# PSUM tiles of a fused attention, gating and mixing kernel: two Vh tiles or two y transposes to one pair of banks, the short Vh tile in one bank, rank-32 additions ahead of the statistics

## The chip, the cores and the metric

The kernel runs on one core of one Trainium2 chip. The core has a matrix engine (TensorE, PE in the profile, with its weight loads as PEld), VectorE (DVE), ScalarE (ACT), GpSimd (POOL) and a queue that issues the DMAs (SyncE, SP). Each engine works through its own instructions in order and waits on semaphores for the others. The metric is device microseconds (us) of one execution. Before the change three executions gave 1314.13, 1310.84 and 1314.26 us, the median 1314.13 us.

## The reference

Eight batches of 576 rows and 512 columns go through three blocks, all in fp32:

- linear attention: `q_s` and `k_s` are softmaxes (of q along the head's 64 columns, of k along the 576 rows), `kv = k_s.T @ v` for each of 8 heads, `x = q_s @ kv`;
- a gated block: `h = gelu(x @ w_in)`, split into `u` and `v` of 512 columns each; `v` is normalised along its columns (mean and variance, then `g_ln`), mixed along the rows by `w_sg` with the bias `b_sg`, multiplied by `u`, sent through `w_out` and added to `x`; call the result `y`;
- a mixing block: `u2 = y + (y.T @ U @ V).T`, where U is 576 by 32 and V is 32 by 576 (the rank-32 addition), and `out = u2 + relu(u2 @ w_ch1) @ w_ch2`.

## The kernel before

fp32 products are made of three matmuls of reduced-precision operands (a high and a low part of each side). `prod` issues the three for both halves of 288 columns, `mm` is one matmul. Every operand therefore has a copy (high part, mostly ACT) and a subtraction (low part, DVE or POOL).

The first part loops over the batches b = 0 to 7. For each b the matrix engine does, in this order: the Vh tiles (`emit_Vh`, the second half of `x @ w_in`, five row tiles t = 0 to 4, the last with 64 rows), mixed with what is left of batch b-1: the transposes of its `y` (`emit_yT`, tile 2 after Vh 0, tiles 3 and 4 after Vh 1), its product with U (`emit_U`, after Vh 2) and the rank-32 addition (`emit_PV`, column blocks 0 and 1 after Vh 3, 2 and 3 after Vh 4); then the maximum over k for batch b+1 (`k_max`, transposes into `pm`), four blocks of `emit_Uh` with `k_spread` (two matmuls into `pb`) ahead of the third, four of `emit_S` (the mixing along the rows), `emit_kv` and `emit_qT` of batch b+1, four of `emit_y`, and `emit_xT` of batch b+1. The second part, from about 634 us on, is the big product with `w_ch1` and `w_ch2`, in a scheme with seven products in place of eight.

After Vh of a tile, ACT applies gelu (L616) into `ge`; `stats` (L622 to L630) takes mean and variance on DVE and the power -0.5 on POOL; `emit_ln` (L632 to L647) makes `sh` on DVE (L636), the normalised tile on ACT (L639), its high part `vh` on ACT and its low part `vl` on POOL. For the short tile a copy of 64 rows (L618) and a DVE addition come before gelu (L620). `emit_ln` of tile t-1 comes after `stats` of tile t. `k_max` makes `mx` from `pm` on DVE (L425), `mh` and `ml` from it, and two `diag` tiles on POOL (DVE for the first batches) which `k_spread` multiplies.

PSUM has eight banks of 2 KB a partition. The pool `ps2` holds three tiles of two banks (tag "big"), `ps1` two tiles of one bank. A new tile takes the place of the one three (or two) allocations before it, and its first matmul waits until all readers of that one are done. Before the change every Vh tile and the y transposes of tiles 2 and 3 take one whole "big" place each, though they fill one of its banks. The order in ps2 for b > 0 is: Vh 0, yT 2, Vh 1, yT 3, Vh 2, Vh 3, addition 0, addition 1, Vh 4, addition 2, addition 3, Uh 0.

The orders of PE (whole kernel) and of DVE (inside the loop) are as written in the program. The orders of ACT, POOL and SP inside the loop are chosen by a planner that simulates the program when it is built; it may put a later instruction of the program ahead of an earlier one that isn't ready. `behind(dve)` only places the k and q maxima behind an earlier DVE instruction.

Of the kernel before, what the change touches and what calls it, by code (L numbers as in the profile page):

```python
# [8 lines left out]
F32 = mybir.dt.float32  # L9
# [13 lines left out]
def fused_kernel(tc, q, k, v, w_in, g_ln, w_sgT, b_sg, w_out, U, V, w_ch1, w_ch2, outT):  # L23
    nc = tc.nc
    B, S, C = q.shape
    P = 128
    H, D = 8, 64
    NT = S // P
    R = S - NT * P
    NC = C // P  # L30
    F = w_out.shape[0]
# [19 lines left out]
    def mm(out, lhsT, rhs, first, last, onto=False):  # L51
        pe.matmul(out, lhsT, rhs, start=first, stop=last, skip_group_check=onto)  # L52

    def tt(eng, out, a, b, op):
        return eng.tensor_tensor(out=out, in0=a, in1=b, op=op)  # L55
# [4 lines left out]
    def copy(out, src):  # L60
        return act.activation(out, src, AF.Copy)  # L61

    def low(eng, out, src, hi):
        return tt(eng, out, src, as_f32(hi), ALU.subtract)

    def opened(name, bufs=1, **kw):
        cm = tc.tile_pool(name=name, bufs=bufs, reuse_waits="tile", **kw)
        return cm.__enter__(), lambda: cm.__exit__(None, None, None)
# [8 lines left out]
    ps2, close_ps2 = opened("ps2", 3, space=PSUM)  # L77
    ps1, close_ps1 = opened("ps1", 2, space=PSUM)
# [22 lines left out]
    half = cst.tile([P, 1], F32, name="half")  # L101
# [360 lines left out]
    def q_max(b, t):  # L462
        if t == 0:
            q_s[b] = tmpp.tile([P, NT + 1, H], F32, tag="qm", name="qm")
        dve.tensor_reduce(
            out=q_s[b][0 : TR[t], t], in_=q3(t), op=ALU.max, axis=mybir.AxisListType.X
        )
# [79 lines left out]
    def halves(t):  # L547
        return t[:, :, 0:HS]

    def two(ap):  # L550
        return ap.rearrange("p (j n) -> p j n", n=HS)
# [10 lines left out]
    def behind(eng):  # L562
        return tc.issue_after(last[eng].ins)
# [31 lines left out]

    vh = {}
    ln = {}

    def emit_Vh(b, t):
        xh, xl, xr, _ = x_t[b]  # L600
        pv = ps2.tile([P, 1024], F32, tag="big", name="pv")[:, 0:F]
        wv_h, wv_l = wi[1]
        for kc in range(NC):
            if t < NT:
                a, l = xh[:, kc, t * P : (t + 1) * P], xl[:, kc, t * P : (t + 1) * P]
                mm(pv, a, wv_h[:, kc], kc == 0, False)
                mm(pv, a, wv_l[:, kc], False, False)
                mm(pv, l, wv_h[:, kc], False, kc == NC - 1)
            else:
                a = xr[:, kc].rearrange("p j r -> p (j r)")  # L610
                mm(pv, a, wv_h[:, kc], kc == 0, False)
                mm(pv, a, wv_l[:, kc], False, kc == NC - 1)
        ge = tmpp.tile([P, F], F32, tag="ge", name="ge", bufs=3)
        ln[b, t] = ge
        if t < NT:
            act.activation(ge, pv, AF.Gelu_apprx_tanh)  # L616
        else:
            copy(ge[0:R], pv[64 : 64 + R])  # L618
            tt(dve, ge[0:R], pv[0:R], ge[0:R], ALU.add)
            act.activation(ge[0:R], ge[0:R], AF.Gelu_apprx_tanh)  # L620

    def stats(b, t):  # L622
        ge, n = ln[b, t], TR[t]
        bst = tmpp.tile([P, 6], F32, tag="bst", name="bst", bufs=3)
        mv = tmpp.tile([P, 2], F32, tag="mv", name="mv", bufs=3)
        dve.bn_stats(out=bst[0:n], in_=ge[0:n])  # L626
        dve.bn_aggr(out=mv[0:n], in_=bst[0:n])
        dve.tensor_scalar(out=mv[0:n, 1:2], in0=mv[0:n, 1:2], scalar1=1e-6, scalar2=None, op0=ALU.add)
        tt(pool, mv[0:n, 1:2], mv[0:n, 1:2], half[0:n], ALU.pow)
        ln[b, t] = (ge, mv)  # L630

    def emit_ln(b, t):  # L632
        ge, mv = ln.pop((b, t))
        n = TR[t]
        shift = tmpp.tile([P, 1], F32, tag="sh", name="sh", bufs=4)
        dve.scalar_tensor_tensor(  # L636
            out=shift[0:n], in0=mv[0:n, 0:1], scalar=-1.0, in1=mv[0:n, 1:2], op0=ALU.mult, op1=ALU.mult
        )
        act.activation(ge[0:n], ge[0:n], AF.Identity, bias=shift[0:n], scale=mv[0:n, 1:2])  # L639
        h = wrk.tile([P, F], F32R, tag=f"vh{t}", name=f"vh{t}")  # L640
        if t < NT:
            l = wrk.tile([P, F], F32R, tag=f"vl{t}", name=f"vl{t}")
            copy(h, ge)
            low(pool, l, ge, h)
            vh[b, t] = (h, l)
        else:
            copy(h[0:R], ge[0:R])  # L647
            low(dve, h[64 : 64 + R], ge[0:R], h[0:R])
            vh[b, t] = h
# [57 lines left out]
    def emit_yT(b, t):  # L707
        n = TR[t]
        if t not in (2, 3) or b == B - 1:
            pt = ps1.tile([P, C], F32, tag="ps1", name="pt1")  # L710
        else:
            pt = ps2.tile([P, 1024], F32, tag="big", name="pt1")[:, 0:C]
        for c in range(NC):
            pe.transpose(pt[0:n, c * P : (c + 1) * P], y_t[b][:, c, t * P : t * P + n], ident)  # L714
        h = wrk.tile([P, C], F32R, tag=f"vh{t}", name=f"yh{t}")
        if t < NT:
            l = wrk.tile([P, C], F32R, tag=f"vl{t}", name=f"yl{t}")
            copy(h, pt)
            low(dve, l, pt, h)
            yn[b, t] = (h, l)  # L720
        else:
            copy(h[0:R], pt[0:R])
            low(dve, h[64 : 64 + R], pt[0:R], h[0:R])
            yn[b, t] = (h,)
# [5 lines left out]
    def emit_U(b, t):  # L730
        if t == 0:
            pu_t[b] = ps1.tile([P, C], F32, tag="ps1", name="pp")
        parts = yn.pop((b, t))
        w = u_w[:, t].rearrange("p a r -> p (a r)")
        for i, y in enumerate(parts):
            mm(pu_t[b], w, y, t == 0 and i == 0, t == NT and i == len(parts) - 1)
        if t == NT:
            pp = pu_t.pop(b)
            if b < B - 1:
                s = tmpp.tile([P, S], F32R, tag="gt", name="pst")[:, 0:C]  # L740
            else:
                s = wrk.tile([P, C], F32R, tag="xr", name="pst")
            copy(s, pp)
            low(dve, s[3 * RK : P], pp[3 * RK : P], s[3 * RK : P])
            pu_t[b] = s
# [10 lines left out]
    def emit_PV(b, c):  # L756
        s = pu_t[b][:, c * P : (c + 1) * P]
        pw = ps2.tile([P, 2, 512], F32, tag="big", name="pw")
        for j in range(2):
            mm(pw[:, j, 0:HS], s, v_w[:, j * HS : (j + 1) * HS], True, True)  # L760
        y = y_t[b][:, c]
        tt(dve, two(y), halves(pw), two(y), ALU.add)
        sp.dma_start(u2d[:, c, :, b * HS : (b + 1) * HS].rearrange("j p n -> p j n"), two(y))
# [360 lines left out]
    def slot(s):  # L1124
        if isinstance(s, int):
            more(s)
            return
        for ch in s:
            if ch == "T":
                more(1)  # L1130
            elif not gate and at[0] > 0:
                if ch == "L":
                    load_ahead()
                elif {"B": at[0] + 3, "S": at[0] + 1, "M": at[0], "H": at[0], "P": idx["H"] - 1, "W": idx["P"] - 1}[ch] >= idx[ch]:
                    op(ch)
# [134 lines left out]
    for b in range(B):  # L1270
# [12 lines left out]
            load_ahead()  # L1283
        for t in range(NT + 1):
            emit_Vh(b, t)
            if nxt:
                with behind(dve):
                    for t2 in Q_MAX[b > 0][t]:
                        q_max(nxt, t2)
                    for _ in range(FOLDS[b > 0][t]):  # L1290
                        next(fold)
            if t < NT:
                stats(b, t)
            slot(TURNS[b][0][t])
            if t > 0:
                emit_ln(b, t - 1)
            if t == NT:
                stats(b, t)
            if b > 0:
                for t2 in ((2,), (3, 4), (), (), ())[t]:  # L1300
                    emit_yT(b - 1, t2)
            if t == 2 and b > 0:
                for t2 in range(NT + 1):
                    emit_U(b - 1, t2)
            if b > 0:
                for c in ((), (), (), (0, 1), (2, 3))[t]:
                    emit_PV(b - 1, c)

        spread_at = 2 if b else 3
        if nxt:  # L1310
# [92 lines left out]
        if nxt:  # L1403
# [3 lines left out]
            emit_xT(nxt, 1)  # L1407
            slot(xs[1])
            emit_yT(b, 0)
            slot(xs[2])  # L1410
            emit_xT(nxt, 2)
            emit_xT(nxt, 3)
            slot(xs[3])
            emit_yT(b, 1)
            slot(xs[4])
        else:
# [116 lines left out]
```

## Time and profile before

| | |
|---|---|
| runs | 1314.13, 1310.84, 1314.26 us; median 1314.13 us |
| the profiled execution | 1313.29 us; span 1311.5 us |
| busy, share of the span | PE 96%, PEld 87%, DVE 75%, ACT 50%, POOL 26% |
| batches 1 to 6 | some 69 to 70 us each |
| second part | 634 to 1311.5 us, PE busy 671.9 us of 677.5 |
| mean granted clock of TensorE | 0.993 of full speed |

The span runs from the first to the last instruction; what the execution takes beyond it (1.8 us) lies around it. In rows of the timeline the first number is the start in us, the second how long the row took in us, then engine, line, operation, output and inputs by the program's names; "x4" counts instructions merged into one row, and a bracket gives the idle time of the engine before the row and who ended it.

### The profile page before, as it was taken

To read this page: it belongs to the slowest core of one execution; us is meant where nothing else is said; L and a number is where in the kernel's file an instruction comes from. 1 tells how busy PE (TensorE), PEld (TensorE's weight loads), DVE (VectorE), ACT (ScalarE), POOL (GpSimd) and SP (SyncE) were. 2 spreads that over 40 slices of the span, in tenths; PEclk is the share of its full clock that TensorE was granted. 3 is DMA by queue.
4 is the path that set the end of the run, shared out by engine and by line. 5 is a ranking of instruction groups with operands and counts; after the bars stand their busy time and mean duration, and the time that the engine had idled before them with its cause. 6 is when DMAs were issued, how large, how long until landed. Compare 5 with 4: busy or idle time off the path is not lost.

```text
span 1311.5 us, 20618 instructions
## 1 busy us (share of the span) xinstructions
PE 1261.5 (96%) x7576; PEld 1137.7 (87%) x7576; DVE 982.4 (75%) x1426; ACT 654.9 (50%) x997; POOL 346.2 (26%) x440
## 2 busy tenths in 40 slices
PE   4799999999999999998999999999999999999998
PEld 2598998989898989888788888888888889999998
DVE  8898979798897979779668953598337963694485
ACT  3756757565766666655454522444134422451342
POOL 3743253633434253666340202000010002000000
PEclk9999999999999999998999999999999999999999
DMA  7525162533425261468998677678766788898886
GB/s 249 166 62 171 37 189 66 171 124 120 142 100 170 76 189 67 156 226 280 322 357 306 227 239 258 209 240 289 258 194 225 245 286 296 275 307 303 261 291 213
DMA packets 135908, 274.15 MB, mean 209 GB/s; under 512 B 15232, under 2 KB 56704, under 8 KB 135808
## 3 DMA queue, kind: packets, MB, share of 16 engines
q1 hardware_dynamic: 135808, 272.84, 63.0%
q8 instruction: 60, 0.98, 0.3%
q14 instruction: 40, 0.33, 0.1%
HBM read 224.56 MB, written 48.23 MB: 208 GB/s over the span
## 4 chain that ended last, share of the span: by engine, by line
PE 72%; DVE 14%; DMA 5%; ACT 3%; POOL 3%; issue 3%; SPq 0%; DVEq 0%; POOLq 0%; ACTq 0%
PE mm L52 50%; PE pv L52 5%; PE pS L52 4%; PE pu L52 4%; PE py L52 3%; DMA stg<-in_w_ch_dram 2%; PE pm L52 1%; DMA qt<-in_q_dram 1%; DVE qt L55 1%; DVE f L187 1%; PE pp L52 1%; POOL chw L55 1%; DVE gt L681 1%; DVE bst L626 1%; PE pt L714 1%
## 5 line engine op out<-in xcount | busy, mean ns | idle before, releaser
L52 PE MATMUL mm<-oh,wu 128*128 128x512 f32 (+1 forms) x1120 | 320.5, 367 | 0.0
L52 PE MATMUL mm<-uh,wu 128*128 128x512 f32 (+1 forms) x1064 | 303.6, 366 | 1.7 <-DVE h L55 0.8
L52 PEld LDWEIGHTS mm<-oh,wu 128*128 128x128 f32 x1120 | 207.1, 188 | 26.3
L52 PEld LDWEIGHTS mm<-uh,wu 128*128 128x128 f32 x1064 | 196.4, 188 | 26.8 <-DVE h L55 1.0
L52 PE MATMUL mm<-ol,wu 128*128 128x512 f32 (+1 forms) x560 | 205.5, 367 | 0.0
L61 ACT ACTIVATE oh<-h 128x1024 fp32r<-128x1024 f32 (+1 forms) x140 | 135.2, 973 | 124.8 <-PE mm L52 102.4
L52 PE MATMUL mm<-ul,wu 128*128 128x512 f32 (+1 forms) x532 | 194.7, 366 | 0.0
L55 DVE TENSOR_TENSOR ol<-h,oh 128x1024 fp32r<-128x1024 f32 (+1 forms) x140 | 155.4, 1113 | 41.0 <-ACT oh L61 40.1
L55 POOL TENSOR_TENSOR ust<-ust 128x1024 f32<-128x1024 f32 (+1 forms) x16 | 36.3, 2276 | 389.8 <-DMA ust<-u2d 349.8
L55 DVE TENSOR_TENSOR h<-mm,u 128x1024 f32<-128x1024 f32 (+1 forms) x57 | 63.3, 1111 | 88.1 <-PE mm L52 88.1
L52 PEld LDWEIGHTS mm<-ol,wu 128*128 128x128 f32 x560 | 105.1, 188 | 13.0
L55 DVE TENSOR_TENSOR u<-mm,u 128x1024 f32<-128x1024 f32 (+1 forms) x53 | 58.9, 1111 | 76.7 <-PE mm L52 72.0
L52 PEld LDWEIGHTS mm<-ul,wu 128*128 128x128 f32 x532 | 99.9, 188 | 12.0
L55 POOL TENSOR_TENSOR chw<-f,chw 128x256 fp32r<-128x256 f32 x98 | 78.4, 816 | 89.6 <-ACT chw L61 84.6
L55 DVE TENSOR_TENSOR h<-h,h 128x1024 f32<-128x1024 f32 (+1 forms) x80 | 88.9, 1112 | 0.0
L1057 ACT ACTIVATE h<-mm 128x1024 f32<-128x1024 f32 (+1 forms) x19 | 17.8, 937 | 131.8 <-PE mm L52 131.8
L1048 ACT ACTIVATE h<-h 128x1024 f32<-128x1024 f32 (+1 forms) x60 | 58.1, 968 | 33.6 <-DVE h L55 33.6
L61 ACT ACTIVATE u<-mm 128x1024 f32<-128x1024 f32 (+1 forms) x24 | 22.5, 938 | 103.4 <-PE mm L52 87.2
L61 ACT ACTIVATE chw<-f 128x256 fp32r<-128x256 f32 x112 | 42.7, 411 | 59.5 <-DVE f L188 22.1
L175 POOL TENSOR_SCALAR stg<-stg 128x256 f32<-128x256 f32 (+1 forms) x83 | 43.4, 527 | 89.8 <-DMA stg<-in_w_ch_dram 48.1
L52 PE MATMUL py<-gh,wo_h 128*128 128x288 f32 x256 | 57.8, 308 | 3.6 <-DVE gt L681 2.4
L52 PE MATMUL py<-gl,wo_h 128*128 128x288 f32 x256 | 56.6, 304 | 4.2 <-DVE gl L55 4.2
(174 smaller groups left out, 2695.2 us busy)
## 6 DMA issues: line engine op xcount, KB each, us to landing
wu<-wd SPq DMA_DIRECT2D x280, 512.0 KB, 4.4
wd<-chw SPq DMA_DIRECT2D x112, 256.0 KB, 3.5
stg<-in_w_ch_dram SPq DMA_DIRECT2D x64, 256.0 KB, 3.8
u2d<-yt SPq DMA_DIRECT2D x32, 288.0 KB, 2.3
vt<-in_v_dram SPq DMA_DIRECT2D x32, 256.0 KB, 6.7
qt<-in_q_dram SPq DMA_DIRECT2D x7, 1024.0 KB, 7.0
kt<-in_k_dram SPq DMA_DIRECT2D x7, 1024.0 KB, 7.0
res<-u2d SPq DMA_DIRECT2D x12, 512.0 KB, 5.0
```

The source lines that it names most:

```text
L52: pe.matmul(out, lhsT, rhs, start=first, stop=last, skip_group_check=onto)
L55: return eng.tensor_tensor(out=out, in0=a, in1=b, op=op)
L61: return act.activation(out, src, AF.Copy)
L175: eng.tensor_scalar(out=hi, in0=hi, scalar1=F64_MOST, scalar2=-F64_MOST, op0=ALU.min, op1=ALU.max)
L187: dve.tensor_scalar(out=b, in0=b, scalar1=3, scalar2=None, op0=ALU.logical_shift_left)
L626: dve.bn_stats(out=bst[0:n], in_=ge[0:n])
L681: dve.scalar_tensor_tensor(out=two(gt), in0=halves(pS), scalar=gl[:, f : f + 1], in1=two(bb), op0=ALU.mult, op1=ALU.add)
L714: pe.transpose(pt[0:n, c * P : (c + 1) * P], y_t[b][:, c, t * P : t * P + n], ident)
L1048: act.activation(h, h, AF.Relu)
L1057: act.activation(h_out(j, 11, n), bank, AF.Relu)
```

## The change

The Vh tiles 0 and 1 share one "big" place, a bank each, and so do tiles 2 and 3; the short tile 4 takes a bank of `ps1`. The y transposes of tiles 2 and 3 share one place in the same way (the last batch's go to `ps1` as before). The order in ps2 for b > 0 becomes: Vh 0 and 1, yT 2 and 3, Vh 2 and 3, addition 0, 1, 2, 3, Uh 0.

The evacuation of a Vh tile (gelu, or copy, addition and gelu for tile 4) is now a function of its own, `gelu_Vh`. For b > 0 it is called after the rank-32 additions of that t, so that on DVE additions 0 and 1 come ahead of `stats` of tile 3, and additions 2 and 3 ahead of tile 4's addition, `sh` of tile 3 and `stats` of tile 4. The order of PE's matmuls is the same as before.

```diff
+    banks = {}
+
+    def bank(key, half, name):
+        if half == 0:
+            banks[key] = ps2.tile([P, 2, 512], F32, tag="big", name=name)
+        return banks[key][:, half]
 
     def emit_Vh(b, t):
         xh, xl, xr, _ = x_t[b]
-        pv = ps2.tile([P, 1024], F32, tag="big", name="pv")[:, 0:F]
+        if t < NT:
+            pv = bank("pv", t % 2, "pv")
+        else:
+            pv = ps1.tile([P, C], F32, tag="ps1", name="pv")
+        ln[b, t] = pv
...
+    def gelu_Vh(b, t):
+        pv = ln[b, t]
         ge = tmpp.tile([P, F], F32, tag="ge", name="ge", bufs=3)
...
-            pt = ps2.tile([P, 1024], F32, tag="big", name="pt1")[:, 0:C]
+            pt = bank("yt", t % 2, "pt1")
...
             emit_Vh(b, t)
+            if b == 0:
+                gelu_Vh(b, t)
             if nxt:
...
+            if b > 0:
+                for c in ((), (), (), (0, 1), (2, 3))[t]:
+                    emit_PV(b - 1, c)
+                gelu_Vh(b, t)
             if t < NT:
                 stats(b, t)
...
-            if b > 0:
-                for c in ((), (), (), (0, 1), (2, 3))[t]:
-                    emit_PV(b - 1, c)
```

## Rows read from the trace of the kernel before

**Rows 1.** The page's busy times: us, share of the span, instructions

```profile
PE 1261.5 (96%) x7576; PEld 1137.7 (87%) x7576; DVE 982.4 (75%) x1426; ACT 654.9 (50%) x997; POOL 346.2 (26%) x440
```

**Rows 2.** Waits of PEld: who for whom; us in total, times, longest

```profile
PEld pw L52 <- DVE yt L55: 5.5, 14, 1.0
PEld py L52 <- DVE gl L55: 4.7, 2, 3.2
PEld pv L52 <- ACT ge L616: 3.0, 6, 0.7
PEld pu L52 <- DVE ge L55: 2.2, 6, 1.3
```

**Rows 3.** Timeline of PE in batch 1, from addition 0 to k_spread

```profile
135.20 0.69 PE L52 MATMUL pw<-v_w,pst 128*128 128x288 f32 x4
136.11 0.51 PE L52 MATMUL pv<-wih,xr 128*128 128x512 f32 x1 [0.22 <-ACT ge L616]
...
138.10 1.20 PE L52 MATMUL pw<-v_w,pst 128*128 128x288 f32 x4
...
139.69 0.54 PE L52 MATMUL pu<-xh,wih 128*128 128x288 f32 x2
...
146.19 0.63 PE L52 MATMUL pb<-diag,ones 128*128 128x512 f32 x2
```

**Rows 4.** Timeline of DVE in the same stretch

```profile
136.09 0.69 DVE L626 BATCH_NORM_STATS2 bst<-ge 128x6 f32<-128x512 f32 x1 [0.47 <-ACT ge L616]
...
137.29 1.42 DVE L55 TENSOR_TENSOR yt<-pw,yt 128x576 f32<-128x576 f32 x2
138.95 0.68 DVE L55 TENSOR_TENSOR ge<-pv,ge 64x512 f32<-64x512 f32 x1 [0.24 <-ACT ge L61]
139.56 1.26 DVE L636 SCALAR_TENSOR_TENSOR sh<-mv 128x1 f32<-128x1 f32 x1
...
141.74 1.41 DVE L55 TENSOR_TENSOR yt<-pw,yt 128x576 f32<-128x576 f32 x2
143.07 0.67 DVE L425 TENSOR_REDUCE mx<-pm 128x4 f32<-128x512 f32 x1
```

**Rows 5.** Timeline of ACT in the same stretch

```profile
135.46 0.60 ACT L616 ACTIVATE ge<-pv 128x512 f32<-128x512 f32 x1 [0.50 <-PE pv L52]
137.29 0.82 ACT L639 ACTIVATE ge<-ge,sh,mv 128x512 f32<-128x512 f32 x1 [1.24 <-DVE sh L636]
138.32 0.59 ACT L61 ACTIVATE ge<-pv 64x512 f32<-64x512 f32 x1 [0.22 <-PE pv L52]
138.82 0.62 ACT L61 ACTIVATE vh<-ge 128x512 fp32r<-128x512 f32 x1
```

**Rows 6.** Timeline of POOL in the same stretch

```profile
139.52 1.29 POOL L55 TENSOR_TENSOR vl<-ge,vh 128x512 fp32r<-128x512 f32 x1 [1.64 <-ACT vh L61]
141.96 0.55 POOL L55 TENSOR_TENSOR mv<-mv,half 64x1 f32<-64x1 f32 x1 [1.15 <-DVE mv L628]
142.48 1.29 POOL L55 TENSOR_TENSOR vl<-ge,vh 128x512 fp32r<-128x512 f32 x1
144.03 1.04 POOL L55 TENSOR_TENSOR diag<-ident,mh 128x512 fp32r<-128x512 f32 x1 [0.26 <-DVE mh L428]
145.03 1.04 POOL L55 TENSOR_TENSOR diag<-ident,ml 128x512 fp32r<-128x512 f32 x1
```

**Rows 7.** Timeline of PE in batch 2, the first matmul of Vh 2

```profile
197.80 0.50 PE L52 MATMUL pv<-wih,xh 128*128 128x512 f32 x1 [1.02 <-DVE yl L55]
```

**Rows 8.** Timelines of DVE and POOL in batch 7, tile 4's shift

```profile
563.75 2.72 DVE L636 SCALAR_TENSOR_TENSOR sh<-mv 64x1 f32<-64x1 f32 x1
...
563.09 1.28 POOL L55 TENSOR_TENSOR vl<-ge,vh 128x512 fp32r<-128x512 f32 x1
```

**Rows 9.** Timelines of PE and ACT in batch 1, Vh 1's start and gelu of Vh 0

```profile
123.88 0.47 PE L52 MATMUL pv<-wih,xh 128*128 128x512 f32 x1
...
124.92 0.60 ACT L616 ACTIVATE ge<-pv 128x512 f32<-128x512 f32 x1
```

## The prediction, made before the changed kernel was run

> **What bounds the kernel now.** I read the page's busy times first: PE is busy 96% of the span [rows 1], so a gain must come out of PE's idle time or not at all. Then the waits of PE's weight loads, which say what PE stands for. The Vh stage has three kinds that recur in every batch from 1 on: an addition's matmuls (`pw`) for an earlier addition on DVE, 5.5 us in 14 waits, two a batch; the short Vh tile (`pv`) for gelu of tile 3, 3.0 us in 6; the first Uh block (`pu`) for the short tile's addition on DVE, 2.2 us in 6 [rows 2]. All three are waits for a PSUM place, and the change removes what they wait for. A fourth, `py` for `gl`, 4.7 us in 2, lies near the end of batch 7 and is DVE's doing. So the pool of time is some 10 us. Last I read the timelines of the four engines from addition 0 to `k_spread`, to see what PE meets when it comes earlier.
>
> In batch 1 PE issues four `pw` matmuls from 135.20, starts the short tile at 136.11, additions 2 and 3 at 138.10, Uh 0 at 139.69 and the `pb` matmuls of `k_spread` at 146.19 [rows 3]. The two `diag` tiles that `pb` multiplies end on POOL at 145.07 and 146.07 (145.03 + 1.04) [rows 6]. So `pb` begins 0.12 us after the second one ends; its second matmul, which is the one that reads it, starts one 512-column interval (0.23 us) later. PE has about 0.2 us to spare there. I looked at the same place in batches 2 to 6 and it repeats: one case stands for six.
>
> **The change part by part, batch 1 to 6.** *PE.* Without its wait the short tile follows four intervals of 0.13 us behind 135.20 (0.13: 48 Uh matmuls between 139.69 and 146.19, less a restart of about 0.11), that is at 135.72; eight intervals of 0.23 us (from 136.11 to 138.10) put additions 2 and 3 at 137.55, and Uh 0 at 138.5. No place is waited for: addition 2 needs gelu 3, done at 136.06 [rows 5]; addition 3 needs addition 0, Uh 0 needs addition 1, both below. `pb` would be due at 144.9 instead of 146.19: the gain on PE alone is 1.3 us a batch.
>
> *DVE.* It is free at 135.62 (136.09 less 0.47 idle) [rows 4]. New order: addition 0 at 135.7 (when its `pw` is out), 0.68 us later addition 1, free at 137.09 (the pair takes 1.42, the next can start 0.06 before its end). Statistics and shift of tile 3's turn take 1.20 us (136.09 to 137.29), so additions 2 and 3 start at 138.29, the short tile's addition at 139.65 (before: 138.95), the shift `sh` 0.61 later at 140.26 (before: 139.56).
>
> *POOL holds the shift.* In the rows the shift takes 1.26 us, from 139.56 to 140.82, and ends with POOL's `vl`, 139.52 to 140.81 [rows 4, 6]; it is an instruction of one column. `vl` follows tile 2's normalisation on ACT, which starts 1.0 us later than before (138.3 against 137.29), since its shift now stands behind additions 0 and 1. The copy of the short tile, ready by 137.9, I take to go ahead of it on ACT, as ACT is idle then; so `vh` comes right behind at 139.17 and `vl` runs from 139.87 to 141.16. The held shift ends at 141.16, 0.34 later than before.
>
> *From the shift to `pb`.* Before, 0.92 us of statistics, then two additions of 1.33 us together (141.74 to 143.07) and `mx`; now `mx` follows the statistics at 142.1, 0.97 us earlier, and `mh` would let POOL begin `diag` at 143.06. But POOL first has the power of the short tile and the next `vl`, in this order in the rows: 141.96 and 142.48 become 142.3 and 142.8, and `vl` ends at 144.07 where it ended at 143.77. Before, POOL stood 0.26 us idle ahead of `diag`; now `diag` starts at 144.07 against 144.03. So the `diag` tiles come when they came before, PE waits for them from 144.9 on, and the second `pb` matmul starts at 146.16 (0.05 after the tile, 0.11 lost between the two) against 146.42. Of 1.3 us, 0.2 to 0.26 us is left. I take 0.2 for each of six batches, 1.2 us. With ACT's other order (normalisation ahead of the copy) `vl` starts at 140.22 and all behind it 0.35 us later: -0.12 a batch. Ends: -0.6 (that, and POOL's power behind `vl` as well, 0.5 more) and +1.3.
>
> *Batch 2's extra wait.* Vh 2 stood 1.02 us for a y transpose's place [rows 7]; with the pair that goes. But it comes ahead of the same chain: DVE runs without idle time from the q maxima on, and `pb` waits for DVE and POOL, so it is worth 0 (upper end 1.1).
>
> *Batch 0* has no additions, and DVE's order is the same: 0. *The second part*, PE busy throughout, is untouched: 0.
>
> *Batch 7* has no `k_spread`, so PE gains there all of its waits, some 2.5 us. But PE then stands for `gl` [rows 2], and DVE's work before that starts from the short tile's shift, 2.72 us long at 563.75 beside POOL's `vl` of 563.09 and what follows it [rows 8]; the loads of the next stage take over the buffers that this tile's `ge` frees. The additions now come ahead, but POOL's queue ahead of and behind that point stays as long. I take 0. Ends: +2.5 (the shift finds POOL free) and -1.
>
> *Shared places.* That a bank of a pair is written while the other is read, no row of before shows. I take it to cost nothing, as the banks are two tiles' worth of separate addresses; the other end is the third rival. The PSUM page of the Trainium skill ("PSUM — Partial Sum Buffer", section "PSUM bank collisions raise a hardware error") says that two engines on different banks run clean and only the same bank and quadrant must be kept apart; no run here shows it. By that rule the sum stays as it is; if the dependencies went by tiles, it would be the rival's.
>
> Sum: 6 x 0.2 = 1.2 us off the profiled execution's 1313.29, 1312.1; that execution lies 0.84 under the median of the runs, so 1314.13 - 1.2 = 1312.9 us.
>
> **The rivals.**
>
> *The full gain.* POOL's order is the planner's. If it puts the `diag` tiles ahead of `vl`, they start at 143.06 and end at 145.1, `pb`'s second matmul is due at 145.13, and each of six batches gains 1.2 us: 7.2 us, 1306.9. With ACT's other order 0.9 a batch, 1308.7. For it: `diag` would now be ready only 0.3 us after `vl` (143.06 against 142.8), where before it came 1.5 us later (144.0 against 142.5), so a small difference in the planner's times turns the order. Against it: in all six batches of the trace `vl` goes first, and it is earlier in the program.
>
> *POOL's queue gets longer.* ACT's other order, and the power behind `vl`: -0.6 in six batches, 1317.7. For it: the power and `vl` become ready within 0.5 us of each other. Against: in the rows the power goes first [rows 6].
>
> *The pair is released and tracked as one tile* (the other side). Place: Vh 1, whose bank lies beside Vh 0's. If its first matmul waits for gelu of Vh 0, PE stands in batch 1 from 123.88 to 125.52 (124.92 + 0.60) [rows 9], 1.7 us with a restart. It decides wherever ACT loads its gelu table after Vh 0, as it does in each of batches 1 to 7: about 1.7 x 7 = 12 us, less 1.2: 1325. For it: buffers here are released by tile. Against: Uh, S and the second part write the two banks of one tile in turn with no such wait, though there no reader stands between.
>
> **How the numbers follow.** A difference of 0.3%, 3.9 us, is about what a measurement of this kernel can tell from no change. Forecast 0.55 (own range 1309.5 to 1315.5, from +2.5 in batch 7 and the two orders on ACT): within 0.50, faster 0.03, slower 0.02. Full gain 0.31: faster 0.29, within 0.02. Longer POOL queue 0.08: within 0.05, slower 0.03. Pair as one tile 0.06: slower. Together faster 0.32, within 0.57, slower 0.11. The range must hold most of the full gain and of the longer queue: 1305.5 to 1317.5.
>
> **What would show it.** In the changed kernel's waits `pw` for `yt`, `pv` for gelu and `pu` for `ge` should be gone or nearly so in batches 1 to 6, and in their place a wait of PE for POOL's `diag` of about 1 us a batch appears. `mx` should start about 1 us earlier against addition 0, `diag` should not. DVE's additions should stand ahead of the statistics with about 0.1 us of idle time. Batches 1 to 6 should be as long as before to a few tenths. The prediction is wrong if POOL's `diag` comes ahead of `vl` (then no wait at `pb`, and some 7 us), if Vh 1 waits for gelu of Vh 0, or if batch 7's stand for `gl` shrinks by more than 2.5 us.

## The result: slower by 1.3%, and the profile after

| | before | after |
|---|---|---|
| median (range) | 1312.99 us (1310.84 to 1314.26) | 1329.7 us (1326.7 to 1331.55) |
| ratio | 1 | 1.0129, 95% interval [1.0115, 1.0142] |
| profiled execution, its span | 1313.29, 1311.5 us | 1330.18, 1328.4 us |
| mean granted clock | 0.993 | 0.984 |

The time is 17 us above the forecast of 1312.9 us and 12 us outside the range. Nearly all of it has arisen when the second part begins: its first matmul starts at 650.49 us instead of 633.92 (+16.6), and the span ends 16.9 us later. The page's busy line answers to [rows 1]: PE is busy only 3.9 us longer, so most of the loss is idle time of PE.

```profile
PE 1265.4 (95%) x7576; PEld 1141.2 (86%) x7576; DVE 989.1 (74%) x1426; ACT 639.2 (48%) x985; POOL 347.6 (26%) x440
```

The waits of PE's weight loads after, to be held against [rows 2] (total us, times, longest):

```profile
PEld pv L52 <- ACT ge L629: 9.6, 9, 3.3
PEld pb L52 <- POOL diag L55: 9.2, 12, 1.2
...
PEld py L52 <- DVE gl L55: 6.7, 3, 3.9
...
PEld pt L727 <- DVE yl L55: 4.6, 4, 3.4
PEld mm L52 <- DVE yt L55: 4.0, 1, 4.0
```

The three waits that the change was to remove are gone: no `pw` for `yt`, no `pu` for `ge`, and the `pv` for gelu is another one. That one is the first reading. PE and ACT in batch 1, against [rows 9]:

```profile
127.82 0.50 PE L52 MATMUL pv<-wih,xh 128*128 128x512 f32 x1 [1.44 <-ACT ge L629]
```
```profile
125.87 1.28 ACT L629 ACT_TABLE_LOAD   x1
127.17 0.60 ACT L629 ACTIVATE ge<-pv 128x512 f32<-128x512 f32 x1
```

Vh 1 has a bank that nobody uses, and starts 0.05 us after the end of gelu of Vh 0 (127.17 + 0.60), which reads the bank beside it. Batch 2 shows the same at 197.36 (gelu ends at 197.31), and so does the pair of y transposes there. PE first, then DVE:

```profile
203.33 1.30 PE L727 MATMUL pt<-ident,yt 128*128 128x128 f32 x8 [2.94 <-DVE yl L55]
204.28 0.78 PE L52 MATMUL pv<-wih,xh 128*128 128x512 f32 x1
204.86 0.63 PE L52 MATMUL pv<-wil,xh 128*128 128x512 f32 x1
```
```profile
202.59 0.68 DVE L55 TENSOR_TENSOR yl<-pt,yh 128x512 fp32r<-128x512 f32 x1
```

The transposes of tile 3, in the second bank of the place, start 0.06 us after DVE's subtraction of tile 2 (202.59 + 0.68) has read the first. Behind the wait a Vh matmul takes 0.63 us and not 0.39: the chip has lowered TensorE's clock. Busy time and granted clock of the stretch before, during and behind it (the columns: length, busy us of PE, PEld, DVE, ACT and POOL with counts, granted clock as a part of 2.4 GHz, share of the DMA engines, GB/s):

```profile
200.50:203.90 3.40, 0.57 (x5) 0.57 (x6) 3.33 (x8) 0.52 (x1) 0.56 (x1) 1.00 1.14 312
203.90:207.30 3.40, 3.40 (x12) 2.79 (x11) 3.27 (x8) 1.89 (x3) 0.55 (x1) 0.53 0.30 72
207.30:211.00 3.70, 3.70 (x17) 2.92 (x17) 2.44 (x6) 1.20 (x3) 0.98 (x1) 0.97 0.00 0
```

In the row with the wait PE is busy for 0.57 us; in the row behind it the granted clock is 0.53 (the level of 1.2 GHz), in the third 0.97. From Vh 2's start to the product with U PE takes 4.34 us there and 2.87 before, so the slow clock costs 1.47 us on top of the wait. The last reading is the end of the first part; PE, then DVE, then the granted clock behind the wait:

```profile
646.08 0.69 PE L52 MATMUL pw<-v_w,pst 128*128 128x288 f32 x4
650.49 0.74 PE L52 MATMUL mm<-uh,wu 128*128 128x512 f32 x2 [3.72 <-DVE yt L55]
```
```profile
648.96 1.48 DVE L55 TENSOR_TENSOR yt<-pw,yt 128x288 f32<-128x288 f32 x3
```
```profile
651.10:654.50 3.40, 3.40 (x10) 2.66 (x9) 0.00 (x0) 0.00 (x0) 0.00 (x0) 0.52 0.56 202
```

The same place in the kernel before, PE and DVE:

```profile
633.92 0.73 PE L52 MATMUL mm<-uh,wu 128*128 128x512 f32 x2 [0.79 <-DVE h L55]
```
```profile
635.31 1.48 DVE L55 TENSOR_TENSOR yt<-pw,yt 128x288 f32<-128x288 f32 x3
```

There `mm` began at 633.92, while the same three additions ran only from 635.31 to 636.79: it did not need them.

One thing in the profile no reading of mine had looked for: ACT's order, which the planner chooses, changed too. The table of ACT's functions for gelu is loaded (`ACT_TABLE_LOAD`, 1.28 us each) ahead of gelu of Vh 0 in every batch before, but in batches 0 and 1 alone after. In all, 40 table loads became 28. Loads at the line of gelu before, after, and in the run with Vh pairs told of below (total us, mean ns, idle us before):

```profile
L616 ACT ACT_TABLE_LOAD x8 | 10.3, 1283 | 0.1
```
```profile
L629 ACT ACT_TABLE_LOAD x2 | 2.6, 1283 | 0.0
```
```profile
L629 ACT ACT_TABLE_LOAD x8 | 10.3, 1283 | 0.1
```

How the delay grows, by the start of the product with U (first `pp`) in each batch, in us. The columns "short tile alone" and "with Vh pairs" are runs told of below, the last column is their difference. Each column is one execution:

| batch | before | after | after - before | short tile alone | with Vh pairs | difference |
|---|---|---|---|---|---|---|
| 1 | 130.32 | 134.30 | 3.98 | 131.00 | 133.69 | 2.69 |
| 3 | 269.90 | 279.11 | 9.21 | 270.38 | 273.71 | 3.33 |
| 5 | 408.80 | 420.56 | 11.76 | 407.63 | 413.27 | 5.64 |
| 7 | 548.64 | 562.78 | 14.14 | 547.35 | 555.58 | 8.23 |
| first `mm` | 633.92 | 650.49 | 16.57 | 633.77 | 643.20 | 9.43 |

### The profile page after: what moved, and what is told of

Read it like the earlier page. It is cut to its first block, busy times and chain, and to the rows that moved or that the text cites. A ratio compares the mean times of both kernels' runs of the same rounds, so it can differ in the third digit from the quotient of the medians.

```text
span 1328.4 us, 20615 instructions
## 1 busy us (share of the span) xinstructions
PE 1265.4 (95%) x7576; PEld 1141.2 (86%) x7576; DVE 989.1 (74%) x1426; ACT 639.2 (48%) x985; POOL 347.6 (26%) x440
## 4 chain that ended last, share of the span: by engine, by line
PE 72%; DVE 17%; DMA 3%; issue 3%; POOL 3%; ACT 2%; SPq 0%; DVEq 0%; POOLq 0%; ACTq 0%
PE mm L52 51%; PE pv L52 5%; PE pS L52 4%; PE py L52 4%; PE pu L52 2%; DVE yt L55 2%; DVE qt L55 1%; PE pp L52 1%; DVE f L187 1%; DMA stg<-in_w_ch_dram 1%; DVE kt L55 1%; DVE gl L55 1%; DVE qs L480 1%; DVE f L188 1%; DVE gt L694 1%
```

## The experiments

Theory: a pair is waited for as one tile (the third rival), and the order costs about nothing. Rival: the places are free, and the new order, or what it does to DVE and POOL, costs it all. Ratios are to the kernel before, timed beside each run (0.001 is 1.3 us); brackets are 95% intervals.

**The change taken apart.** `e1_own_places` is the change without pairs (each Vh tile and y transpose has a whole place again), the short tile and the order stay:

```diff
-            pv = bank("pv", t % 2, "pv")
+            pv = ps2.tile([P, 1024], F32, tag="big", name="pv")[:, 0:F]
...
-            pt = bank("yt", t % 2, "pt1")
+            pt = ps2.tile([P, 1024], F32, tag="big", name="pt1")[:, 0:C]
```

> The changed kernel with its pairs undone: every Vh tile of 128 rows and the y transposes of tiles 2 and 3 on a two-bank place of their own, the short tile in one bank and the additions ahead of the statistics as changed. Theory (a pair's second bank waits for the readers of its first, since dependencies go by tiles): the waits of Vh 1 for gelu of Vh 0 and of the y transposes for yl go, some 8 us, and the end's wait of the first large product for the last addition goes too, some 3 us, since the count of places shifts the last addition to another place; PE still waits for POOL's diag at k_spread; 1315 to 1319 us. Rival (the order of the additions costs the time, through k_spread): 1326 to 1330 us.

Measured 1319.07 us, 1.0056 [1.004, 1.0072]: at the upper end of the theory.

`e2_pairs_only` keeps pairs and short tile, with gelu and additions in the old order:

```diff
-            if b == 0:
-                gelu_Vh(b, t)
+            gelu_Vh(b, t)
...
-            if b > 0:
-                for c in ((), (), (), (0, 1), (2, 3))[t]:
-                    emit_PV(b - 1, c)
-                gelu_Vh(b, t)
```

> The pairs and the short tile's single bank alone, the additions behind the statistics as before. Theory: Vh 1's wait for gelu of Vh 0 stays (0.5 to 1.7 us a batch) and so does the end's wait of 3 us, the wait of k_spread for diag shrinks; 1320 to 1327 us. Rival (order): 1311 to 1315 us.

Measured 1325.5 us, 1.0105 [1.0081, 1.0129], as the theory had it.

`e3_order_only` has the new order with every tile's place as before, `e4_short_only` only the short tile in a single bank (`ps1.tile([P, C], F32, tag="ps1", name="pv")`).

> The order of the additions alone: they stand ahead of the statistics on DVE, all tiles on places of their own as before. Theory: no wait of Vh 1 for gelu of Vh 0, k_spread waits for diag by up to 1 us a batch; 1312 to 1317 us. Rival (order): 1324 to 1330 us.

> The short Vh tile in a single bank alone. Theory and rival: about as before, 1310 to 1315 us; a gain of up to 0.5 us a batch where the short tile no longer waits for gelu of tile 3, as far as k_spread does not take it back.

Measured 1317.67 us, 1.005 [1.0032, 1.0067], just above the range of the first theory, and 1309.9 us, 0.999 [0.9979, 1.0001]. So the short tile alone costs nothing; pairs on top of it cost 0.0115 (15 us), the order on top of it 0.0066 (8.7 us). Both theories hold a part, and together they cost less than their sum (0.0139 of 0.0181). One reason stands in the traces: the runs with the order in all batches, `e1`, `e3` and the change, have 28 table loads on ACT, `e2` and `e4` in the old order 40. With the loads, PE waits 13.6 us for gelu at the pairs (`e2`), without them 9.6 (the change). How much of the 0.0042 that is, no run shows.

**Which pair.** `e15_vh_pairs` and `e16_yt_pair` add to `e4_short_only` one kind of pair each (one of the two `bank(...)` lines).

> Old order, short tile in one bank, only the Vh tiles in pairs; the y transposes have whole places. Theory (Vh 1 and Vh 3 wait for gelu of their pair's first half, some 0.5 us in each batch, and y transposes cost the rest): 1315 to 1319 us, PE's wait of pv for gelu about 10 us, no wait of pt for yl in batch 2 above 1 us. Rival (all of the 15.6 us of both pairs is in the Vh pairs): 1323 to 1327.

> Old order, short tile in one bank, only the y transposes of tiles 2 and 3 in a pair; the Vh tiles have whole places. Theory (the second transpose waits for the subtraction of the first, 3 us in batch 2 and little elsewhere): 1313 to 1317 us, wait of pt for yl 2 to 3 us once, none of pv for gelu. Rival (this pair costs nothing alone): 1309 to 1311.

Measured 1324.26 us, 1.0102 [1.0087, 1.0118], and 1313.32 us, 1.001 [0.9998, 1.0023]. For the Vh pairs the rival was right: nearly all is in them. Weight loads of the run with Vh pairs, and of the one with the y pair:

```profile
PEld pv L52 <- ACT ge L629: 14.1, 9, 3.3
...
PEld mm L52 <- DVE yt L55: 4.0, 1, 4.0
```
```profile
PEld pt L727 <- DVE yl L55: 8.6, 9, 2.8
```

The y pair waits 8.6 us in nine waits, where I had expected 2 to 3 us once, and costs some 2.6 us (0.002; the interval touches that of the short tile alone). Part of its wait replaces one of the short tile's run, where Vh 2 stands for `yl` (2.0 us in 2); where the rest went is not shown. The table's last column shows the Vh pairs' share: 0.6 to 1.7 us at Vh 1 of each batch from 1 on, 8.9 in all, less what is won back; the stand at the end (`mm` for `yt`) comes on top.

**The pair's partner.** `e5_far_pairs` is the change with Vh 0 beside Vh 2, and 1 beside 3:

```diff
-            pv = bank("pv", t % 2, "pv")
+            pv = bank(("pv", t % 2), t // 2, "pv")
```

> The changed kernel with other partners in the pairs: Vh 0 with Vh 2 and Vh 1 with Vh 3, as many places and banks as before this edit. Theory (a pair's second bank waits for all readers of its first): gelu of the partner is long done, so the waits of Vh for gelu go, and with them PE's slower clock after them; 5 to 9 us less than the changed kernel, 1320 to 1325 us. The y transposes' wait for yl in batch 2 and the wait at the end for the last addition stay. Rival (sharing places as such, or fewer of them, costs the time): 1327 to 1331 us.

Measured 1324.24 us, 1.0089 [1.0064, 1.0114]. Its waits:

```profile
PEld pb L52 <- POOL diag L55: 11.4, 12, 1.2
...
PEld py L52 <- DVE gl L55: 8.2, 3, 4.3
PEld pt L727 <- DVE yl L55: 7.4, 8, 2.3
...
PEld pv L52 <- ACT ge L629: 0.6, 1, 0.6
```

Only the partner was changed, and `pv` for gelu falls from 9.6 us in 9 waits to 0.6 in one. The wait follows the pair and no bank: it is the tracking by tile. But the time does not follow the wait. `pb`, `py` and `pt` take up part of it (9.2 to 11.4, 6.7 to 8.2, 4.6 to 7.4), and, against my expectation, the stand at the end is gone as well. What that stand costs (0.0042, below) is as much as this run gains (0.0040), so the waits at Vh 1 by themselves are worth nothing that these runs can tell once the order is there.

**The end of the first part.** PE's stand of 3.7 us ahead of the second part was in no forecast of mine. `e6_last_add` gives the very last addition two single banks in place of a big place (`last_PV(b, c)` for c = 3 too); `e12_end_adds` puts six conversions of weights on DVE behind the last additions (`slot(STEP_TURNS[6])` moved behind `pvs(6)`).

> The changed kernel with the very last rank-32 addition (batch 7, block 3) in two single banks, as blocks 0 to 2 are, in place of a two-bank place. Theory (the number of places allocated before the end decides which place the last addition gets, and the first large product needs place 0): the wait of about 3.7 us at the start of the large products goes, 1325 to 1328 us. Rival (the wait is DVE being behind, whatever the place): 1328 to 1331 us.

> The changed kernel with the conversion pieces of the seventh step behind the last addition on DVE, not ahead of it. Theory (the first large product waits for the last addition, which stands on DVE behind six conversion instructions): PE's wait of 3.7 us goes down to about 1 us, 1326 to 1328 us. Rival (the place and not the order decides): 1328 to 1331 us.

Measured 1326.24 us, 1.0105 [1.0088, 1.0122], and 1326.09 us, 1.0111 [1.0094, 1.0128]; each interval overlaps that of the change (1.0129). In the first the wait only moved (`pw` for `yt`, 3.4 us in 2), in the second it fell to 2.7. Both say that PE waits for late additions, neither why it must. In the compiled programs the last addition lies in PSUM banks 2 and 3 before the change and in 0 and 1 after it and in the run with Vh pairs, in 2 and 3 again with the far pairs (where PE shows no such wait), and the second part's first product lies in 0 and 1 in all of them. Which of the three places a tile gets is the allocator's choice when the program is built (not always the one three allocations back, as the section on the kernel says), and the pairs shift it. `e17_after_turn` turns it once more in the changed kernel, with a matmul into an unused place. `e18_before_turn` makes the clash in the kernel before, with three transposes into the three places ahead, so that the first product gets banks 2 and 3:

```diff
+                        skip = ps2.tile([P, 2, 512], F32, tag="big", name="skip")
+                        mm(skip[:, 0, 0:HS], pu_t[b][:, 0:P], v_w[:, 0:HS], True, True)
                         emit_PV(b, c)
```
```diff
+    for _ in range(3):
+        skip = mmp.tile([P, 2, 512], F32, tag="mm", name="mm")
+        pe.transpose(skip[:, 0, 0:P], ident, ident)
     p2["ps"] = lambda: mmp.tile([P, 2, 512], F32, tag="mm", name="mm")
```

> The changed kernel with one matmul of 288 columns more, into an otherwise unused big place ahead of the very last addition; it turns the places by one, so that the last addition no longer gets the two banks that the second part writes first. Theory (PE's wait of mm for yt at the end of the first part is that shared place): that wait is gone, 1325 to 1327 us, 3 to 4 below the changed kernel. Rival (PE waits there for late work of DVE whatever the places): the wait stays near 3 us, 1328 to 1331.

> The kernel before with three transposes of 128 columns more, into three unused places of the second part's pool, so that the second part's first product gets the two banks of the last addition. Theory (the same shared place, made in the kernel without pairs): a wait of mm for yt of 3 to 4 us appears, 1314.5 to 1316.5 us. Rival (the pairs are needed for it): no such wait, 1311 to 1313.

Measured 1323.03 us, 1.0087 [1.007, 1.0104], and 1315.38 us, 1.0029 [1.0016, 1.0042]. PE at the end of the first part, in the changed kernel with the turn, then in the kernel before with the clash, and the granted clock behind that clash:

```profile
641.83 0.43 PE L52 MATMUL pw<-v_w,pst 128*128 128x288 f32 x2
642.10 0.69 PE L52 MATMUL mm<-uh,wu 128*128 128x512 f32 x2
```
```profile
632.66 0.33 PE L1453 MATMUL mm<-ident 128*128 128x128 f32 x1 [0.79 <-DVE h L55]
634.92 0.44 PE L1453 MATMUL mm<-ident 128*128 128x128 f32 x2 [1.93 <-DVE yt L55]
635.58 1.22 PE L52 MATMUL mm<-uh,wu 128*128 128x512 f32 x2 [0.23 <-DVE yt L55]
```
```profile
635.60:638.60 3.00, 3.00 (x7) 2.42 (x8) 0.00 (x0) 0.00 (x0) 0.00 (x0) 0.50 0.75 271
```

One matmul more, and the changed kernel loses the wait and 0.0042 (5.5 us, more than the 3.7 of the wait, as the clock behind it had been at 0.52), some 2 us more than the theory had. The clash costs the kernel before 0.0029 (3.8 us). Its stand looks different, though: 0.79 us of it is the wait for `h` that the kernel before has too, 1.93 us falls on the second transpose, which waits for earlier additions in its own place, and only 0.23 us on the product.

Here single executions can mislead. The programs of `e6`, `e12` and `e17` are the changed kernel's up to the last step of batch 7, and still they reach batch 7's first `pp` of the table at 560.84, 560.35 and 557.02 us against 562.78. So equal work differs by up to 5.8 us between two profiles, and the table's columns are no finer than that. The edited stretch itself, from the start of batch 7's own product with U (the last `pp`, behind the table's) to the span's end, takes 693.3 us in the changed kernel and 688.2 with the turn, 690.3 in the kernel before and 693.4 with the clash. By the times and by this stretch, that cause is settled.

**The order's cost.** At `k_spread`, `e7_spread_later` (the change) and `e8_short_spread` (on the short tile alone) put it a block of Uh later, `spread_at = 3`, with its subtractions behind it.

> The changed kernel with k_spread one Uh block later in batches 1 to 6 (ahead of the fourth block in place of the third, and the k subtractions behind it). Theory (POOL's diag is late for k_spread and takes back what the additions' order gives): PE's wait for diag goes, 1.2 us or more in each of six batches, 1318 to 1323 us. Rival (what the order costs lies in DVE's own work and comes out elsewhere): 1327 to 1331 us.

> The short tile's single bank alone, and k_spread one Uh block later. Theory: the 0.57 us a batch that PE gains ahead of k_spread is no longer given back there (0.47 us); 3 us less than with the short tile alone, 1306 to 1308 us. Rival: as the short tile alone, 1309 to 1311 us.

Measured 1350.0 us, 1.0289 [1.0274, 1.0305], and 1335.52 us, 1.0177 [1.0162, 1.0193]: far off every theory. `pS` now waits for `gt` on DVE, in the second of them

```profile
PEld pS L52 <- DVE gt L694: 13.5, 6, 3.4
```

against 0.3 us in the short tile's run. The k subtractions on DVE need `pb`, and all that follows them in DVE's order comes late. So `pb` can't be given time by moving it; its inputs must come earlier. `e9_short_kmax`, `e10_own_kmax` and `e11_after_kmax` do that: in batches 1 to 6 the k maxima go ahead of Vh 4, on the short tile alone, on the order with own places and on the change:

```diff
+            if t == NT and b > 0 and nxt:
+                k_max(nxt)
             emit_Vh(b, t)
```

> The short tile's single bank alone, and in batches 1 to 6 k_max (its four transposes, mx, mh, ml and diag) one step earlier, ahead of Vh 4 and of the additions 2 and 3 on DVE. Theory (k_spread waits for POOL's diag, which stand at the end of the chain over tile 3's and 4's statistics): diag are ready some 4 us earlier, PE keeps the 0.57 us a batch that it gains ahead of k_spread: 3 us less than the short tile alone, 1305 to 1308 us. Rival (what PE gains there comes out as another wait for DVE later in the batch): as the short tile alone, 1309 to 1311 us.

> Additions ahead of the statistics and the short tile in a single bank, no pairs, and k_max one step earlier in batches 1 to 6. Theory: PE's wait for diag (5.1 us in 12) goes, and the order's gain of 1.1 us a batch ahead of k_spread stays: 1308 to 1312 us, against 1319 without the earlier k_max. Rival: 1316 to 1320 us.

> The changed kernel with k_max one step earlier in batches 1 to 6. Theory: its waits for diag at k_spread (5.9 us in 12, and a slower clock after two of them) go, 1319 to 1323 us; the waits of Vh 1 for gelu and the end's wait stay. Rival: 1327 to 1331 us.

Measured 1316.63 us, 1.0037 [1.0024, 1.005]; 1313.8 us, 1.002 [1.0006, 1.0034]; 1326.59 us, 1.011 [1.0095, 1.0126]. With the old order the maxima delay additions 2 and 3 (`pu` for `yt` 10.0 us in 11 against 3.5 in 8), a miss. With the new one no `pb` for `diag` is left, yet `e10` was above its forecast and `e11` too. One reason for `e11` is in its trace: with the early maxima ACT has its 40 table loads again, and PE's wait for gelu at the pairs rises from 9.6 to 15.0 us. In `e10` the first `pp` in batch 7 is 4 us ahead of the kernel before (544.62 against 548.64), the first `mm` 0.4 behind (634.34): batch 7 gives it back. `e13_kmax_b7` and `e14_own_b7` therefore run batch 7 in the old order, with and without the early maxima:

```diff
-            if b > 0:
+            if 0 < b < B - 1:
                 for c in ((), (), (), (0, 1), (2, 3))[t]:
                     emit_PV(b - 1, c)
                 gelu_Vh(b, t)
```

> The kernel with own places and the k maxima early, but batch 7 in the old order (gelu right behind each Vh tile, additions behind the stage's other work). Theory (what the early maxima gain in batches 1 to 6, some 5 us, is lost in batch 7 because the additions there come ahead of the statistics): 1306 to 1309 us, PE's wait of py for gl back to about 4 us. Rival (batch 7 only passes on what comes late from batch 6, whatever the order inside it): 1312 to 1315, the wait of py for gl stays above 6 us.

> The order with own places and the short tile in one bank, batch 7 in the old order. Theory (some 5 us of the order's 9 lie in batch 7): 1313 to 1315 us. Rival (the cost lies in batches 1 to 6, at k_spread): 1318 to 1320 us, as with the new order throughout.

Measured 1310.82 us, 0.9996 [0.9983, 1.0009], between theory and rival, and 1315.51 us, 1.0036 [1.0024, 1.0048], 0.5 us above the theory. Waits of `e14_own_b7`, then of `e13_kmax_b7`:

```profile
PEld pb L52 <- POOL diag L55: 8.5, 12, 1.2
...
PEld py L52 <- DVE gl L55: 5.2, 2, 3.2
```
```profile
PEld py L52 <- DVE gl L55: 5.3, 3, 3.2
```

The old order in batch 7 is worth 0.0020 (`e1` to `e14`) or 0.0024 (`e10` to `e13`), some 3 us: in each pair the intervals overlap, but both give the same, and `py` for `gl`, 8.4 us in both `e1` and `e10`, falls to 5.2 and 5.3. From `e14` to `e13` it is 0.0040 (5.2 us), clear of noise. I put it down to the wait at `pb`: in `e14` PE itself stands 5.1 us there in 12 waits, and 1.54 us more go with a half clock behind one of them in batch 5. ACT's table loads go from 28 to 40 between these two as well, and no run parts the two. With both out, the new order costs nothing and gains nothing: no version beats the kernel before beyond its interval.

**The account.** Of 0.0129: the clash of places at the end 0.0042 (the change to `e17`), the pairs' waits otherwise 0.0031 (`e17` to `e1`; the two intervals just touch), the order in batch 7 0.0020 (`e1` to `e14`), the early maxima 0.0040 (`e14` to `e13`, put down to the wait at `pb`), the rest about 0 (0.9996). The first and the last of the four are clear of noise by themselves. In the old order the pairs weigh more (0.0115): there ACT loads its table ahead of gelu of Vh 0 in every batch.

## Why the prediction was wrong, point by point

- **"Shared places ... I take it to cost nothing": the step that failed first.** I argued with addresses, where the program's dependencies go by tiles. The pairs cost 0.0073 with the new order (the change against `e1`, some 10 us) and 0.0115 with the old one. The third rival named place and cause (Vh 1 behind gelu of Vh 0), and got 0.06. Its time, 1325, was for Vh 1 alone, with a table load ahead of gelu in each of seven batches. In the run with Vh pairs, which keeps the loads, Vh 1's starts add some 9 us over seven batches against its 12; in the changed kernel they add 4.7 (1.68 in batch 1, about 0.5 after, where no load stands ahead of gelu). That the measured time lies as near to 1325 as it does is luck. What filled up the difference I had nowhere: the transposes' 2.94 us in batch 2, a half clock behind it, the end, and the order's own cost. The cited rule of the Trainium skill ("PSUM — Partial Sum Buffer", section "PSUM bank collisions raise a hardware error"), that different banks run clean, was not put to the test for the two banks of one tile: a dependency kept PE off the second bank until the first had been read.
- **"Batch 2's extra wait ... with the pair that goes" failed.** The place is free, but the pair's other half is not read yet: 1.02 us [rows 7] became 2.94, ahead of the transposes.
- **"Batch 0 ...: 0" failed as well.** Only DVE's order is the same there. Vh 1 stands 2.97 us for gelu of Vh 0 and runs at half clock behind it, Vh 3 stands 1.29 us; the wait for `km` that ends the stage shrinks from 6.96 to 1.10 us and takes back most; 2.25 us are left when Vh 0 of batch 1 starts (122.92 against 120.67).
- **"The second part ... is untouched: 0" failed** for its first product. A changed number of places taken shifts who inherits which banks, which cost 0.0042. I had read no row of that point: [rows 3] to [rows 9] all lie ahead of it.
- **The three old waits went**, as said. In batch 1 the steps can be held against the trace with 3.94 us added, the delay of Vh 1's start (127.82 against 123.88, [rows 9]): short tile 139.66 expected, additions 2 and 3 141.49, Uh 0 142.44. PE after, against [rows 3], with `pb`:

```profile
139.18 0.69 PE L52 MATMUL pw<-v_w,pst 128*128 128x288 f32 x4
139.71 0.40 PE L52 MATMUL pv<-wih,xr 128*128 128x512 f32 x1
...
141.55 0.69 PE L52 MATMUL pw<-v_w,pst 128*128 128x288 f32 x4
...
142.44 0.50 PE L52 MATMUL pu<-xh,wih 128*128 128x288 f32 x2
...
149.29 0.50 PE L52 MATMUL pb<-diag,ones 128*128 128x512 f32 x1 [0.23 <-POOL diag L55]
150.29 0.50 PE L52 MATMUL pb<-diag,ones 128*128 128x512 f32 x1 [0.50 <-POOL diag L55]
```

- **The chain to `diag` held to 0.2 us.** DVE and POOL after, against [rows 4] and [rows 6]:

```profile
143.38 0.67 DVE L55 TENSOR_TENSOR ge<-pv,ge 64x512 f32<-64x512 f32 x1
143.98 1.18 DVE L649 SCALAR_TENSOR_TENSOR sh<-mv 128x1 f32<-128x1 f32 x1
...
146.08 0.67 DVE L425 TENSOR_REDUCE mx<-pm 128x4 f32<-128x512 f32 x1
146.78 1.33 DVE L428 CAST mh<-mx 128x4 fp32r<-128x4 f32 x1
```
```profile
143.85 1.29 POOL L55 TENSOR_TENSOR vl<-ge,vh 128x512 fp32r<-128x512 f32 x1 [1.09 <-ACT vh L61]
146.30 0.54 POOL L55 TENSOR_TENSOR mv<-mv,half 64x1 f32<-64x1 f32 x1 [1.15 <-DVE mv L641]
146.81 1.28 POOL L55 TENSOR_TENSOR vl<-ge,vh 128x512 fp32r<-128x512 f32 x1
148.20 1.04 POOL L55 TENSOR_TENSOR diag<-ident,mh 128x512 fp32r<-128x512 f32 x1
```

  The shift ends at 145.16 (145.10 expected), `mx` starts at 146.08 (146.04), `diag` at 148.20 (148.01), the second `pb` matmul at 150.29 (150.10). One row was missed: `mh`, four columns, takes 1.33 us while `vl` runs on POOL beside it from 146.81 to 148.09, just as the shift did. In the kernel before it took 0.17:

```profile
143.78 0.17 DVE L428 CAST mh<-mx 128x4 fp32r<-128x4 f32 x1
```

  By the Trainium skill, page "SBUF — State Buffer", section "Who interferes with whom", a cast of VectorE can run in a two-port mode, and in that mode it and a GpSimd instruction hold a shared pair of ports one at a time, the other blocked for the whole of it. The trace agrees, as `mh` ends at 148.11 and `vl` at 148.09; which mode the cast ran in no run shows.

  The gain left in batch 1 is 0.07 us and not 0.26. Mis-sized was what the wait does later: in batches 2 and 3 PE stands 0.99 us ahead of the first `pb` matmul and not 0.23, and behind the one in batch 3 the clock is lowered (0.58 from 296.8 to 300.2 us). So the term "0.2 for each of six batches", a gain of 1.2 us, did not come: from the first `pp` of batch 1 to that of batch 7 the order with own places (`e1`) takes 420.1 us and the kernel before 418.3, single executions both. Over the whole kernel the order costs 0.0066 (8.7 us, `e4` to `e1`).
- **The full gain (0.31) was given far too much:** `vl` stayed ahead of `diag`.
- **"Batch 7 ... I take 0, ends +2.5 and -1" had the sign of its likelier end wrong:** PE gains 2.9 us there (1.13 at Uh 0, 1.76 up to `pS`, `e1` against `e14`) and loses 6.0 behind it up to the last product with U, at `py` for `gl` and at the transposes, of which 1.1 come back before the second part. [rows 2] showed that PE waits for DVE there, and the additions were put ahead of DVE's chain.

## What to carry to other kernels

Two tiles in one allocation are one tile to whoever waits: before packing, list the second half's first writer and the first half's last reader, and pack only halves whose reader is done anyway. Here even that won nothing back beyond the end's stand (the far pairs, 1.0089, against 1.0087 with near pairs and the turn). Count what the packing does to the rotation of places up to the next stage's first tile, and look at the banks that the two get. A wait taken from the busiest engine is worth only what the next join leaves: follow its other inputs first, and mind that a stand of PE may cost a second time in the clock behind it. Where a planner orders an engine, compare that engine's order before and after as well; and where two profiles of equal work differ by 5.8 us, trust a difference of that size only from repeated times.

## What the runs showed of the hardware

A stand of PE can be followed by a lower granted clock even in the middle of the kernel: 0.53 in the row behind 2.94 us of waiting, 0.52 behind 3.72, 0.50 behind three waits of 0.79, 1.93 and 0.23 us. In the changed kernel PE's waits at `pb` are alike in batches 2 and 3 (0.99 us, one matmul, then 0.49 and 0.50 us), but behind them the granted clock is 1.00 in batch 2 and 0.58 in batch 3: the length of a stand alone does not decide it. So a wait can cost a second time, 1.47 us on top of 2.94 in batch 2, and in `e14` 1.54 us on top of 0.97 and 0.50 at `pb` in batch 5.

A DVE instruction of four columns took 1.33 us, where it took 0.17 in the kernel before (at 143.78 us, batch 1), when a 512-column subtraction ran on POOL at the time.
